# A planner that writes the instruction order of an attention and feed-forward kernel gets new costs, a replay as its judge, and two more late weight jobs

## The chip, the cores and the metric

One core of a Trainium2 chip runs the whole program, once per launch. The metric is the device time of one launch in microseconds (us), lower is better. TensorE (PE in the profile) does the matmuls, VectorE (DVE), ScalarE (ACT) and GpSimd (POOL) the elementwise work, and nearly every DMA is issued from one queue, that of SyncE (SP). PSUM has eight banks of 128 x 512 float32 values, into which matmuls accumulate.

## The reference, cut to what matters

```python
# q, k, v: (8, 8, 576, 64) float32.   w_in (512, 2048), w_out (2048, 512): float64
scores = q @ k.T / 8                            # per batch and head
mask: heads 0-3: 0 <= i - j < 32
      heads 4-7: 0 <= i - j < 128 and (i - j) % 4 == 0
attn = exp(scores - max);  attn /= attn.sum() + 1e-9
x = (attn @ v)  as 4608 tokens x 512
h = x @ w_in                                    # 4608 x 2048
g = maximum(h, 0) + log1p(exp(-abs(h)))         # softplus
out = g @ w_out                                 # 4608 x 512
```

Each row of scores has 32 live keys, so attention is small; the two matrix products of the feed-forward part are nearly all of the arithmetic.

## The kernel before, in words

**Tiling.** The 4608 tokens are nine chunks of 512 (`c` 0 to 8). A chunk's attention is four groups (a pair of heads each), taken as two *couples* of two groups. Everything is float32, and a large product is made of three matmuls: each factor is split into a high and a low part (`xh`, `xl`; `gh`, `gl`), and high x high, low x high and high x low accumulate in one bank. The splits are a copy with rounding on ACT and a subtraction on DVE. One matmul here is 128 x 128 weights by 512 columns.

**Stages.** (1) An *opening* of some 60 us whose order is written out by hand (`OPENING`). (2) The *early part*: chunks 0 to 2 in 48 slots (chunk, block of 128 of the 2048 hidden units), of which the planner orders slots 10 to 47. A slot is 12 matmuls into a bank `h_ps`, the softplus (three ACT steps, one DVE step), the split into `gh` and `gl`, and two slots later 12 matmuls into four banks `o_ps`. Beside it the weights, which come as float64 words, are decoded on ACT and DVE (`decode`). (3) The *late part*: chunks 3 to 8 as three pairs. For each pair both products are done by seven block products instead of eight (`PRODUCTS`): sums and differences of blocks of x (`s1` to `s4`) against sums and differences of blocks of the weights (`t1` to `t4`). One of 56 *units* of a pair is 12 matmuls into the banks `x`, `y` or `z`; units 0 to 27 (i = 0) are the first product, units 28 to 55 (i = 1) the second. Each unit's weights are one 512 KB tile of a ring of five (`load_ring`, tile `ring`), loaded from DRAM, where stage 2 left them.

**Jobs.** The blocks `t1` to `t4` are made by 16 *jobs* (`job(i, p, stage)`: product i, pair p of weight blocks). A job is two sums of 512 columns and four differences of 256, each of them on POOL or on DVE as the planner finds, then two copies on ACT and two subtractions on DVE (tiles `b`, `d`, `cast`) and four DMAs of 256 KB back to DRAM (`w_t<-cast`). Three jobs (`FIRST_JOBS`) run beside slots of the early part, nine more of stage 1 from the start of chunk 2 on; their `cast` tiles lie where ring tiles 3 and 4 will be. The last `LATE_JOBS` (4) of stage 2 come after `switch`, which hands the early part's memory to the late one; they use one set of tiles (`n1` to `n4`) one after the other, and the split tiles of units 28 to 30 come to lie on the same places.

**Couples.** `weights(n)`: load q and k, 128 small matmuls into one two-bank PSUM tile `att` (a PE *visit*), mask, maximum, 16 exponentials. `turned(n)`: `divisor`, a 32 x 32 transpose on DVE, four DMAs to DRAM and one back (`send`, `bring`; `turned<-sq`, `sq<-turned`). `attended(n)`: 128 small matmuls (a second visit), a division, a transpose, four DMAs out and one in (`send_x`, `bring_x`; `rows<-x_full`, `x_full<-rows`).

**What sets the order.** From slot 10 on, all work is a list of some two thousand `Task`s with an engine, a cost in us, and what it reads and writes. `prioritized` gives each a due time (`latest`), back from the planned begins of the PE chain; `simulated` runs the list, each engine taking the ready task with the earliest due time less its head start (`sooner`); a sum may go to POOL or, at another cost (`other`), to DVE. `blamed` lists the tasks behind each idle stretch of PE, the search gives some of them another head start, 400 times over (`PASSES`), keeps the plan whose simulated end is lowest, and writes the instructions in that order. So each engine runs in the planned order on the chip, and waits where the plan was too hopeful. Some costs carry `port`: DVE and POOL tasks with that mark never overlap in the plan; and a POOL sum that the plan held back gets a real wait on the DVE instruction that was ahead of it (`summed`, L913).

**Costs before.** `COST` gives a fixed part and a part for each column: ACT 0.22 + 0.00079 n, DVE 0.155 + 0.00104 n, POOL 0.05 + 0.00196 n, a PE matmul 0.2275; a DMA takes 0.1 us of SP; the queue moves 0.33 MB per us and lands 2.2 us later; a task on another engine starts 0.2 us after what it needs, on PE 0.6 us, a PE visit 1.5 us.

Of the kernel before, what the change touches and what calls it, by code (L numbers as in the profile page):

```python
# [51 lines left out]
NCP = NPAIR // 2  # L52
PLANNED = OPENED + 1
FIRST_JOBS = 3
LATE_JOBS = 4
RING = 5
NEG = -1.0e9
DEPTH = 8
# [43 lines left out]
def tile_windowed_attention_softplus_ffn(  # L102
# [497 lines left out]
    groups = [Group(c, pr) for c in range(NCH) for pr in range(NPR)]  # L600
# [42 lines left out]
    tiles, ready = {}, {}  # L643
# [202 lines left out]
    def load_unit(u):  # L846
# [4 lines left out]
        load_dma(out=ring[n].bitcast(F32), in_=streamed[i, PRODUCTS[k][1], jj])  # L851

    COST = {
        "PE": 0.2275, "ACT": (0.22, 0.00079), "DVE": (0.155, 0.00104), "POOL": (0.05, 0.00196),
    }
    LAST = len(slots) - 1
    PASSES, DEEP = 400, 12
    END, DMA_RATE, DMA_LATENCY, BACKLOG = 1.0e6, 0.33e6, 2.2, 2.0
    tasks, writer, readers = [], {}, {}

    class Task:
# [25 lines left out]
    def cost_of(engine, *widths):  # L887
        fixed, each = COST[engine]
        return sum(fixed + each * n for n in widths)

    def task(engine, widths, run, *what, reads=(), writes=(), **kw):
        widths = widths if isinstance(widths, tuple) else (widths,)
        return Task(engine, cost_of(engine, *widths), lambda: run(*what), reads, writes, **kw)

    def transfer(run, *what, size, n=1, reads=(), writes=()):
        return Task("SP", 0.1 * n, lambda: run(*what), reads, writes, size=size)

    chain = []

# [33 lines left out]
    TILE = 2 * P * CH * 4  # L933
# [39 lines left out]
    @sooner  # L973
    def weights(n, begun=False):
        x = x_of_couple(n)
        queries = ["q0", "q1"] if begun else [x]
        if not begun:
            transfer(load_queries, n, writes=queries, size=TILE, n=2)
            transfer(load_keys, n, writes=["k0", "k1"], size=TILE, n=3)
        Task("PE", 1.4, lambda: scores(n), [*queries, "k0", "k1"], ["att"], visit=True)  # L980
        for e in range(2):
            gr, s = groups[n + e], both("s") if e == 0 else [("s", 1)]
            task("DVE", (512, 512), gr.maximum, reads=["att"], writes=s)
            s = [("s", e)]
            for t in range(0, NB, 2):
                Task("ACT", 1.07, lambda gr=gr, t=t: gr.exponentials(range(t, t + 2)), (), s)

    @sooner
    def turned(n, begun=False):
        x = x_of_couple(n)  # L990
        if not begun:
            transfer(load_v, n, writes=both("v"), size=TILE)
        transfer(load_v, n + 1, writes=[x], size=TILE)
        for e in range(2):
            task("DVE", (8, 8), groups[n + e].divisor, reads=[("s", e)], writes=[("ri", e)])
            task("DVE", 512, turn, n + e, reads=[("s", e)], writes=[f"q{e}"])
            transfer(send, n + e, reads=[f"q{e}"], writes=[("sent", e)], size=TILE // 2, n=4)
            transfer(bring, n + e, reads=[("sent", e)], writes=[f"q{e}"], size=TILE // 2)

    @sooner  # L1000
    def attended(n):
        x = x_of_couple(n)
        Task("PE", 1.4, lambda: values(n), ["q0", "q1", *both("v"), x], ["att"], visit=True)
        for e in range(2):
            task(
                "DVE", 512, groups[n + e].normalized, reads=["att", ("ri", e)],
                writes=both("v") if e == 0 else [("v", 1)],
            )
        for e in range(2):
            task("DVE", 512, groups[n + e].turn_rows, reads=[("v", e)], writes=[x])  # L1010
        transfer(groups[n].send_x, reads=[x], writes=["rows"], size=TILE, n=4)
        transfer(groups[n].bring_x, reads=["rows"], writes=[x], size=TILE)

    def couples(first, last, begun=False):
# [102 lines left out]
    def decode(ff, i, n):  # L1117
        key = ff, i
        a, w = ("a", n % 3), ("W", ff, i)
        task("ACT", 580, decode_step, *key, 0, reads=[], writes=[a])  # L1120
        for step in (1, 2):
            Task("DVE", 0.425, lambda step=step: decode_step(*key, step), (), [a])
        for step in (3, 4):
            task("DVE", 512, decode_step, *key, step, writes=[a], port=True)
        task("ACT", 512, decode_step, *key, 5, reads=[a], writes=[w])
        task("DVE", 512, decode_step, *key, 6, reads=[a], writes=[w], port=True)

    def early_slot(i):
        c, ff = slots[i]
        turn = i % 2  # L1130
        h, e, gh, gl = ("h", turn), ("early e", turn), ("early gh", turn), ("early gl", turn)
        on_tensor(12, h_unit, i, reads=[("W", ff, 0), *x_keys(c)], writes=[h])
        o_unit(i - LAG)
        task("ACT", (512, 512, 512), activated, i, reads=[h], writes=[e])
        task("DVE", 512, softplus, i, reads=[h], writes=[e])
        task("ACT", 512, g_high, i, reads=[e], writes=[gh])
        task("DVE", 512, g_low, i, reads=[e, gh], writes=[gl], port=True)
# [222 lines left out]
    for i in range(2):  # L1360
        for p in range(NPAIR):
            for b in ("b11", "b21", "b22"):
                transfer(
                    keep_block, i, p, b, reads=[("W", 2 * p, i), ("W", 2 * p + 1, i)], writes=[("D", i, b, p)],
                    size=TILE // 2,
                )
    couples(2 * NPAIR - 8, 2 * NPAIR - 4, True)
    kept_first = slots.index((0, 6)) + LAG
# [1 line left out]
    for i in range(PLANNED, LAST + 1):  # L1370
# [3 lines left out]
        if slots[i] == (2, 0):  # L1374
# [5 lines left out]
            couples(2 * NPAIR - 4, 2 * NPAIR)  # L1380
            for n in range(FIRST_JOBS, 2 * NPAIR - LATE_JOBS):
                sooner(job, JOBS_SOONER)(n // NPAIR, n % NPAIR, 1)
# [5 lines left out]
    for i in range(LAST + 1 - LAG, LAST + 1):  # L1388
# [5 lines left out]
         + both("e0") + both("e1") + [("n", n) for n in range(1, 6)] + [("n", 1, 1)])  # L1394
    for p in range(NPAIR - LATE_JOBS, NPAIR):
        sooner(job, JOBS_SOONER)(1, p, 2)
    for u, (s, i, k, jj) in enumerate(units):
# [10 lines left out]
        else:  # L1408
            x = PRODUCTS[k][0]
# [7 lines left out]
    def simulated():  # L1417
        free = dict.fromkeys(("PE", "POOL", "DVE", "ACT", "SP", "NONE"), 0.0)
        candidates = {e: [] for e in free}
        queue_free = port_free = 0.0  # L1420
        for t in tasks:
            t.left, t.ready, t.chosen = len(t.after), 0.0, None
            if not t.left:
                candidates[t.engine].append(t)
        order = []
        for _ in range(len(tasks)):
            best = None
            for e in free:
                some = candidates[e]
                if e == "DVE":  # L1430
                    some = some + [t for t in candidates["POOL"] if t.other is not None]
                if not some:
                    continue
                begins = [(max(free[e], t.ready, port_free if t.port else 0.0), t) for t in some]
                start = min(b for b, _ in begins)
                if e == "SP":
                    start = max(start, queue_free - BACKLOG)
                t = min((t for b, t in begins if b <= start), key=lambda t: (not t.visit, t.latest - t.sooner))
                if best is None or (start, t.latest - t.sooner) < best[:2]:
                    best = start, t.latest - t.sooner, t, e  # L1440
            start, _, t, e = best
            candidates["POOL" if t.other is not None else e].remove(t)
            order.append(t)
            t.chosen = e
            cost = t.other if t.other is not None and e == "DVE" else t.cost
            t.idle, t.begun, end = start - free[e], start, start + cost
            free[e] = end
            if t.port:
                port_free = end
            if t.size:  # L1450
                queue_free = max(queue_free, end) + t.size / DMA_RATE
                end = queue_free + DMA_LATENCY
            t.done = end
            for other in t.then:
                lag = 0.0 if other.engine == e else 1.5 if other.visit else 0.6 if other.engine == "PE" else 0.2
                other.ready = max(other.ready, end + lag)
                other.left -= 1
                if not other.left:
                    candidates[other.engine].append(other)
        return max(t.done for t in tasks), order  # L1460

    def prioritized(begins):
        for t in tasks:
# [22 lines left out]
    dice = random.Random(0)  # L1486
# [4 lines left out]

    def attempt():
        prioritized(begins)
        return simulated()[0]

    best = None
    for n in range(PASSES):
        tried = begins, [t.sooner for t in tasks]
        end = attempt()
        if best is None or end <= best[0]:  # L1500
            gaps = list(blamed())
            best = end, *tried, [t.begun for t in chain]
# [3 lines left out]
        for idle, late in dice.choices(gaps, weights=[g[0] for g in gaps], k=dice.choice((1, 1, 2))):  # L1506
            step = dice.choice((-5.0, 2.0, 5.0, 10.0, 20.0))
# [6 lines left out]
    taken = None  # L1514
    for t in simulated()[1]:
# [4 lines left out]
        if t.engine == "DVE" and t.port:  # L1520
            taken = pinned[0]
# [118 lines left out]
```

## Time and profile before

| what | us |
|---|---|
| median of three runs | 849.8 (849.76, 849.80, 851.98) |
| the profiled execution, whole | 847.29 |
| its span, first to last instruction | 845.5 |
| TensorE busy (matmuls) | 815.5 |
| VectorE, ScalarE, GpSimd busy | 633.6, 551.5, 253.8 |
| DMA | 218.95 MB, 259 GB/s over the span |

"Busy" counts an instruction from its start to its end as recorded. Ends and starts of neighbours overlap a little, so a chain of instructions is faster than the sum of their durations; and an instruction that waits for a port while it runs is counted busy. "Idle before" is the time that the engine stood still in front of an instruction, with what ended it.

### The profile page before, as it was taken

The numbers are of one execution on the slowest core, as the hardware profiler recorded it, in microseconds if no ns is written. First come the engines' busy times: TensorE is split into PE (matmuls) and PEld (weight loads), VectorE is DVE, ScalarE is ACT, GpSimd is POOL, SyncE is SP. The second block draws the span as 40 slices with busy tenths as digits, with TensorE's granted clock in tenths as the row PEclk, the third lists the DMA queues.
The fourth block names the chain that finished last, engine by engine and source line by source line (L and its number), as shares of the span: only waits on it lengthen the run. The fifth ranks groups of instructions, "written<-read, shape, count | busy, mean of one in ns | idle before, by whom it ended". The sixth has DMA issues, their size and how long they took to land.

```text
span 845.5 us, 19702 instructions
## 1 busy us (share of the span) xinstructions
PE 815.5 (96%) x7834; PEld 654.6 (77%) x7835; DVE 633.6 (75%) x874; ACT 551.5 (65%) x1185; POOL 253.8 (30%) x162
## 2 busy tenths in 40 slices
PE   6799999999999998999998999899999999999998
PEld 4678888888877876788877788688878888888886
DVE  5798898786766764788978867497888685666963
ACT  5687677775766854589976535688873527776341
POOL 0000000014642638563434304032164221322730
PEclk9899999999999999999999999999999999999999
DMA  9599992667887874999889997778778875555563
GB/s 331 182 315 382 336 307 89 193 203 249 287 293 247 282 232 125 328 338 326 295 267 300 350 357 267 282 246 295 242 272 298 295 233 195 199 196 183 195 230 118
DMA packets 118492, 218.95 MB, mean 259 GB/s; under 512 B 11520, under 2 KB 53632, under 8 KB 118400
## 3 DMA queue, kind: packets, MB, share of 16 engines
q1 hardware_dynamic: 117968, 216.97, 75.9%
q8 instruction: 62, 1.02, 0.5%
q10 hardware_dynamic: 432, 0.72, 0.2%
q14 instruction: 30, 0.25, 0.1%
HBM read 162.07 MB, written 55.57 MB: 257 GB/s over the span
## 4 chain that ended last, share of the span: by engine, by line
PE 86%; DVE 4%; DMA 4%; POOL 2%; issue 2%; ACT 1%; SPq 1%; DVEq 0%; POOLq 0%; ACTq 0%
PE y L215 23%; PE x L215 14%; PE z L215 14%; PE h_ps L215 14%; PE o_ps L215 14%; PE a_ps L215 3%; PE s_ps L215 3%; POOL b L913 1%; SPq L150 1%; DMA ring<-w_t 1%; DMA x_full<-rows 1%; DMA raw<-w 1%; DMA v<-vp 1%; POOL x_full L913 1%; DVE sm L423 1%
## 5 line engine op out<-in xcount | busy, mean ns | idle before, releaser
L913 POOL TENSOR_TENSOR g_of<-g_of 128x1024 f32<-128x1024 f32 x48 | 121.7, 2543 | 228.0 <-DVE g L913 135.4
L913 DVE TENSOR_TENSOR g<-g_of,g 128x1024 fp32r<-128x1024 f32 x84 | 127.1, 1526 | 43.0 <-ACT g L929 42.9
L929 ACT CAST g<-g_of 128x1024 fp32r<-128x1024 f32 x84 | 87.9, 1047 | 101.4 <-PE y L215 38.6
L215 PE MATMUL o_ps<-gh,parts 128*128 128x512 f32 x384 | 131.5, 401 | 0.3 <-issue 0.3
L215 PE MATMUL h_ps<-xh,parts 128*128 128x512 f32 x384 | 129.4, 395 | 0.0
L913 POOL TENSOR_TENSOR b<-parts 128x512 f32<-128x512 f32 x32 | 46.3, 1455 | 260.1 <-DVE parts L209 178.5
L215 PE MATMUL y<-g,ring 128*128 128x512 f32 x432 | 102.6, 395 | 2.5 <-DVE g L913 2.1
L1260 ACT ACTIVATE e<-e 128x1024 f32<-128x1024 f32 x96 | 101.8, 1061 | 2.6
L215 PEld LDWEIGHTS y<-g,ring 128*128 128x128 f32 x432 | 80.9, 188 | 22.1 <-DVE g L913 2.5
L215 PEld LDWEIGHTS o_ps<-gh,parts 128*128 128x128 f32 x384 | 72.6, 189 | 18.9 <-issue 0.7
L215 PEld LDWEIGHTS h_ps<-xh,parts 128*128 128x128 f32 x384 | 72.5, 189 | 16.5 <-DVE e L667 0.4
L215 PE MATMUL o_ps<-gl,parts 128*128 128x512 f32 x192 | 76.5, 399 | 2.7 <-DVE gl L682 2.6
L411 ACT ACTIVATE s<-s,nm 128x64 f32<-128x64 f32 x224 | 75.0, 336 | 4.0 <-DVE nm L402 3.9
L215 PE MATMUL h_ps<-xl,parts 128*128 128x512 f32 x192 | 75.3, 392 | 0.0
L215 PE MATMUL z<-g,ring 128*128 128x512 f32 x288 | 68.4, 395 | 1.7 <-DVE g L913 1.7
L215 PE MATMUL x<-g,ring 128*128 128x512 f32 x288 | 69.0, 395 | 0.6 <-issue 0.6
L215 PEld LDWEIGHTS z<-g,ring 128*128 128x128 f32 x288 | 53.9, 188 | 14.7 <-DVE g L913 2.1
L215 PE MATMUL x<-a_h,ring 128*128 128x512 f32 x192 | 64.5, 397 | 0.0
L215 PEld LDWEIGHTS x<-g,ring 128*128 128x128 f32 x288 | 53.7, 188 | 13.4 <-issue 0.8
L215 PE MATMUL z<-s_h,ring 128*128 128x512 f32 x192 | 63.4, 390 | 0.5 <-DVE ob L931 0.5
L215 PE MATMUL y<-s_h,ring 128*128 128x512 f32 x192 | 63.5, 392 | 0.3 <-DMA ring<-w_t 0.3
L913 DVE TENSOR_TENSOR g_of<-y,temp 128x512 f32<-128x512 f32 x60 | 39.2, 682 | 22.0 <-PE y L215 21.9
(96 smaller groups left out, 1518.7 us busy)
## 6 DMA issues: line engine op xcount, KB each, us to landing
ring<-w_t SPq DMA_DIRECT2D x96, 512.0 KB, 4.5
ring<-w_b SPq DMA_DIRECT2D x72, 512.0 KB, 4.4
raw<-w SPq DMA_DIRECT2D x64, 256.0 KB, 5.6
w_t<-cast SPq DMA_DIRECT2D x64, 256.0 KB, 4.4
w_b<-parts SPq DMA_DIRECT2D x48, 256.0 KB, 3.4
v<-vp SPq DMA_DIRECT2D x14, 512.0 KB, 5.3
x_full<-vp SPq DMA_DIRECT2D x14, 512.0 KB, 6.8
turned<-sq SPq DMA_DIRECT2D x112, 64.0 KB, 3.0
```

Source lines behind the costliest of these rows:

```text
L150: ins = tc.keep_in_program_order((engine or nc.sync).dma_start(**kw))
L215: tc.keep_in_program_order(nc.tensor.matmul(**kw))
L411: pin(nc.scalar.activation(out=self.blocks[:, t], in_=src, func=AF.Exp, bias=self.nm[:, t : t + 1], scale=1.0 / 8.0 if self.masked else 1. ...
L423: pin(nc.vector.tensor_scalar(out=sm, in0=sm, scalar1=1.0e-9, scalar2=1.0, op0=ALU.add, op1=ALU.mult))
L913: pin((nc.gpsimd if name == "POOL" else nc.vector).tensor_tensor(out=dst, in0=a, in1=b, op=op))
L929: pin(nc.scalar.copy(out=dst, in_=src))
L1260: pin(nc.scalar.activation(out=to(), in_=of(), func=func, **kw))
```

## The change

Four things change. **Costs** in the planner (`COST`, the exponentials, `divisor`, the first decode steps, the SP time of a DMA, the DMA rate; `divisor` and the first decode steps now carry `port`). **Lags**: 0.12 us on the same engine and 0.18 us across engines, 0.5 us to PE; a PE visit waits between 1 and 3 us after its inputs, by how much time it has (`calm`). **The judge**: a plan's order is run again by `replayed`, each engine in its fixed order, with random extra time on each task, twice, and the search keeps the plan with the lowest mean end of PE. **`LATE_JOBS`** goes from 4 to 6, so that seven jobs stay in stage 1. No instruction is added to or taken from the kernel: the order on each engine, the choice of POOL or DVE for the sums, and the place of two jobs are what can differ.

```diff
-LATE_JOBS = 4
+LATE_JOBS = 6
...
     COST = {
-        "PE": 0.2275, "ACT": (0.22, 0.00079), "DVE": (0.155, 0.00104), "POOL": (0.05, 0.00196),
+        "PE": 0.229, "ACT": (0.09, 0.00084), "DVE": (0.07, 0.00104), "POOL": (0.14, 0.00215),
     }
...
-    PASSES, DEEP = 400, 12
-    END, DMA_RATE, DMA_LATENCY, BACKLOG = 1.0e6, 0.33e6, 2.2, 2.0
+    PASSES, DEEP, SEEDS, CALM = 400, 12, 2, 3.0
+    SPREAD = {"PE": 0.0, "ACT": 0.02, "DVE": 0.02, "POOL": 0.05, "SP": 0.3, "NONE": 0.0}
+    LATE, VISIT = 0.3, 0.0
+    END, DMA_RATE, DMA_LATENCY, BACKLOG = 1.0e6, 0.38e6, 2.2, 2.0
...
-    def transfer(run, *what, size, n=1, reads=(), writes=()):
-        return Task("SP", 0.1 * n, lambda: run(*what), reads, writes, size=size)
+    def transfer(run, *what, size, n=1, each=0.4, reads=(), writes=()):
+        return Task("SP", each * n, lambda: run(*what), reads, writes, size=size)
...
-                Task("ACT", 1.07, lambda gr=gr, t=t: gr.exponentials(range(t, t + 2)), (), s)
+                Task("ACT", 0.67, lambda gr=gr, t=t: gr.exponentials(range(t, t + 2)), (), s)
...
-            task("DVE", (8, 8), groups[n + e].divisor, reads=[("s", e)], writes=[("ri", e)])
+            task("DVE", (8, 180), groups[n + e].divisor, reads=[("s", e)], writes=[("ri", e)], port=True)
...
-        transfer(groups[n].send_x, reads=[x], writes=["rows"], size=TILE, n=4)
+        transfer(groups[n].send_x, reads=[x], writes=["rows"], size=TILE, n=4, each=0.6)
...
-            Task("DVE", 0.425, lambda step=step: decode_step(*key, step), (), [a])
+            Task("DVE", 0.345, lambda step=step: decode_step(*key, step), (), [a], port=True)
...
-        task("ACT", (512, 512, 512), activated, i, reads=[h], writes=[e])
+        task("ACT", (560, 560, 560), activated, i, reads=[h], writes=[e])
...
-                    size=TILE // 2,
+                    size=TILE // 2, each=0.55,
...
-                lag = 0.0 if other.engine == e else 1.5 if other.visit else 0.6 if other.engine == "PE" else 0.2
+                lag = (
+                    0.0 if e == other.engine == "PE" else calm(other, end) if other.visit else 0.5 if other.engine == "PE"
+                    else 0.12 if other.engine == e else 0.18
+                )
...
+    def calm(t, ready):
+        return min(CALM, max(1.0, (t.latest - ready) * 0.15))
+
+    def replayed(order, seed):
+        dice = random.Random(seed)
...
+        for t in order:
+            t.met = t.held = None
+            if t.chosen == "POOL" and t.begun > t.ready + 0.1:
+                t.held = taken
+            if t.chosen == "DVE" and t.port:
+                taken = t
...
+                    for other in t.after if t.held is None else (*t.after, t.held):
...
+                        lag = 0.0 if e == other.chosen == "PE" else 0.2 if "PE" in (e, other.chosen) else 0.12
+                        start = max(start, other.met + lag)
...
+            cost = t.other if t.other is not None and e == "DVE" else t.cost
+            cost = cost * (1.0 + SPREAD[e] * dice.random()) + (LATE if dice.random() < 0.02 else 0.0)
...
+            if t.size:
+                queue_free = max(queue_free, end) + t.size / DMA_RATE
+                end = queue_free + DMA_LATENCY * (1.0 + 0.4 * dice.random())
+            t.met_at, t.met = start, end
+        return free["PE"]
...
     def attempt():
         prioritized(begins)
-        return simulated()[0]
+        order = simulated()[1]
+        return sum(replayed(order, seed) for seed in range(SEEDS)) / SEEDS
```

## Rows read from the trace of the kernel before

**Rows 1.** The page, part 1: busy time by engine, share, instructions.
```profile
PE 815.5 (96%) x7834; PEld 654.6 (77%) x7835; DVE 633.6 (75%) x874; ACT 551.5 (65%) x1185; POOL 253.8 (30%) x162
```

**Rows 2.** Windows by stage: length; busy (count) of five engines; PE clock; DMA share, GB/s.
```profile
56.00:262.00 206.00, 205.96 (x2004) 165.94 (x2006) 164.13 (x285) 147.82 (x366) 37.24 (x36) 1.00 0.80 266
262.00:338.00 76.00, 71.62 (x906) 57.05 (x891) 47.72 (x67) 45.78 (x120) 41.95 (x38) 0.98 0.67 209
338.00:422.00 84.00, 83.15 (x725) 67.50 (x724) 71.54 (x93) 68.77 (x134) 44.98 (x33) 1.00 0.93 323
```

**Rows 3.** PE's waits from 56 us on: total, times, longest, us.
```profile
PE s_ps L215 <- issue: 4.0, 1, 4.0
PE o_ps L215 <- DVE gl L682: 2.6, 1, 2.6
PE a_ps L215 <- DMA sq<-turned: 2.4, 2, 1.5
PE y L215 <- DVE g L913: 2.1, 1, 2.1
PE z L215 <- DVE g L913: 1.7, 1, 1.7
...
PE z L215 <- DVE ob L931: 0.5, 1, 0.5
PE y L215 <- DMA ring<-w_t: 0.3, 1, 0.3
```

**Rows 4.** Windows of 20 us, columns as in rows 2.
```profile
60.00:80.00 20.00, 20.00 (x271) 15.96 (x270) 17.94 (x38) 14.41 (x43) 0.00 (x0) 1.00 1.03 367
...
320.00:340.00 20.00, 17.39 (x70) 13.69 (x69) 10.58 (x10) 10.88 (x17) 17.01 (x14) 0.91 0.43 134
...
460.00:480.00 20.00, 19.39 (x205) 15.51 (x204) 18.42 (x21) 12.93 (x38) 9.61 (x4) 1.00 0.96 346
```

**Rows 5.** Timeline around two waits: start, us, engine, what, [idle before].
```profile
331.42 3.98 POOL L913 TENSOR_TENSOR b<-parts 128x512 f32<-128x512 f32 x2
332.48 1.77 DVE L682 TENSOR_TENSOR gl<-e,gh 128x512 fp32r<-128x512 f32 x1
444.01 7.12 POOL L913 TENSOR_TENSOR g_of<-g_of 128x1024 f32<-128x1024 f32 x3 [2.29 <-ACT g L929]
...
448.96 2.21 DVE L423 TENSOR_SCALAR sm<-sm 128x8 f32<-128x8 f32 x1
```

**Rows 6.** DVE's groups from 56 us on: divisor's first step, count, busy, mean ns.
```profile
L423 DVE TENSOR_SCALAR sm<-sm 128x8 f32<-128x8 f32 x30 | 19.8, 661 | 0.0
```

**Rows 7.** POOL's groups from 56 us on.
```profile
L913 POOL TENSOR_TENSOR b<-parts 128x512 f32<-128x512 f32 x32 | 46.3, 1455 | 260.1 <-DVE parts L209 178.5 <-DVE gl L682 36.3 <-DVE cast L1077 35.8
```

**Rows 8.** ACT's timeline, two neighbours back to back.
```profile
450.15 1.04 ACT L827 CAST a_h<-x_full 128x1024 fp32r<-128x1024 f32 x1
451.10 1.04 ACT L929 CAST g<-g_of 128x1024 fp32r<-128x1024 f32 x1
```

**Rows 9.** SP's timeline around 300 us: DMA issues.
```profile
300.15 5.49 SPq L150 DMA_DIRECT2D turned<-sq  x8
...
308.24 1.19 SPq L150 DMA_DIRECT2D sq<-turned  x2
```

**Rows 10.** POOL's timeline: first two sums of the first late job.
```profile
348.71 2.58 POOL L913 TENSOR_TENSOR b<-parts 128x512 f32<-128x512 f32 x2 [3.44 <-DVE s_l L831]
```

**Rows 11.** DVE's timeline: last subtraction of the last late job.
```profile
397.62 0.68 DVE L1077 TENSOR_TENSOR cast<-b,cast 128x512 fp32r<-128x512 f32 x1
```

**Rows 12.** PE's timeline: first matmuls of unit 28.
```profile
421.38 1.79 PE L215 MATMUL x<-g,ring 128*128 128x512 f32 x7
```

**Rows 13.** DMA from 338 to 422 us: total; issues, KB each, median us to landing.
```profile
DMA packets 11240, 27.15 MB, mean 323 GB/s; under 512 B 1248, under 2 KB 2400, under 8 KB 11232
...
ring<-w_t SPq DMA_DIRECT2D x15, 512.0 KB, 6.1
w_t<-cast SPq DMA_DIRECT2D x20, 256.0 KB, 5.7
```

More of the change, by code (lines that the diff above doesn't have):

```diff
@@ L1460, in simulated @@
         return max(t.done for t in tasks), order
+    def calm(t, ready):
+        return min(CALM, max(1.0, (t.latest - ready) * 0.15))
+    def replayed(order, seed):
+        dice = random.Random(seed)
+        engines = ("PE", "POOL", "DVE", "ACT", "SP", "NONE")
+        free, heads = dict.fromkeys(engines, 0.0), {}
+        queues = {e: [t for t in order if t.chosen == e][::-1] for e in engines}
+        queue_free = port_free = 0.0
+        taken = None
+        for t in order:
[4 more added lines that the diff above has]
+                taken = t
+        left = len(order)
+        while left:
+            best = None
+            for e in engines:
+                if not queues[e]:
+                    continue
+                t = queues[e][-1]
+                if e not in heads:
+                    start = free[e]
+                    for other in t.after if t.held is None else (*t.after, t.held):
+                        if other.met is None:
+                            start = None
+                            break
+                        lag = 0.0 if e == other.chosen == "PE" else 0.2 if "PE" in (e, other.chosen) else 0.12
+                        start = max(start, other.met + lag)
+                    if start is None:
+                        continue
+                    heads[e] = start
+                start = max(heads[e], port_free) if t.port else heads[e]
+                if best is None or start < best[0]:
+                    best = start, e
+            start, e = best
+            del heads[e]
+            t = queues[e].pop()
+            left -= 1
+            cost = t.other if t.other is not None and e == "DVE" else t.cost
+            cost = cost * (1.0 + SPREAD[e] * dice.random()) + (LATE if dice.random() < 0.02 else 0.0)
+            if t.visit:
+                cost += VISIT
+            end = free[e] = start + cost
+            if t.port:
+                port_free = end
+            if t.size:
[3 more added lines that the diff above has]
+        return free["PE"]
     def prioritized(begins):
```

## The prediction

> **What bounds the kernel now.** The first view is the busy time by engine: TensorE is busy 815.5 of 845.5 us [rows 1], so only its idle 30 us and its slow stretches can go. Second, busy time by stage: in the first 206 us under the planner PE is busy 205.96 us, so nothing is to be had there, and things can only go wrong; the idle time lies from 262 us on, 4.4 us of it up to 338 us and 0.85 us in the next 84 [rows 2]. The rest lies in the opening, which the change doesn't touch, behind the last matmul, and in later waits. Third, PE's waits from 56 us on [rows 3]. Seven of them are waits for other engines or transfers: 2.6 for the subtraction `gl`, 2.4 in two visits for the turned squares, 2.1 and 1.7 for splits `g`, 0.5 and 0.3; together 9.6 us. The longest one, 4.0 us, is "issue": it ends on nothing that another engine did, so no plan decides it. Last, the clock: in the slice with the 2.6 us wait the mean granted clock was 0.91 [rows 4]. With levels 1.0 (2.4 GHz) and 0.5 (1.2 GHz) that is 0.09 / 0.5 x 20 = 3.6 us at the low one, after PE had stood still, and costs 1.8 us. A plan can reach 9.6 + 1.8 = 11.4 us.
>
> **Where the waits come from.** POOL and DVE hinder each other: beside a run of POOL's sums a DVE step takes a multiple of its time. POOL's three sums at 444.01 ran 7.12 us, and in them `divisor`'s first step, 8 columns wide, took 2.21 us; `gl` at 332.48 took 1.77 us beside two sums of 3.98 us [rows 5]. Over the run the 30 first steps of `divisor` took 19.8 us, 0.66 each [rows 6]. The old plan prices both steps of `divisor` at 2 x (0.155 + 0.008) = 0.33 us with no port.
>
> **The change part by part.**
> *Prices.* A POOL sum of 1024 columns is 2.06 us by the old line, 2.34 by the new one; the trace has 7.12 / 3 = 2.37 [rows 5]. One of 512: 1.05 old, 1.24 new, 2.58 / 2 = 1.29 in the trace [rows 10], 1.46 in the mean with its waits [rows 7]. An ACT step of 1024: 1.03 old, 0.95 new; neighbours start 451.10 - 450.15 = 0.95 apart [rows 8]. An SP issue: 0.1 old, 0.4 new; eight took 5.49 us, 0.69 each, and two 1.19, 0.60 each [rows 9]. So a `send` with its `bring`, five issues, holds SP for some 3 us where the old plan had 0.5, which is more than the longest wait for squares (1.5) [rows 3, 9]. The plan was hopeful just where PE waited: on POOL, on the port, on SP. It was too cautious on ACT and DVE, and that caution goes: with ACT 8% and DVE some 10% cheaper, work is planned closer to its due time. That costs nothing where DVE has room (164 of 206 us in the first stage [rows 2]); without that cover one wait of the present kind comes there, 9.6 / 7 = 1.4 us, with a clock fall at most 3.2 us. On chip the prices themselves cost nothing: no instruction is added.
> *Visits.* They are put 1 to 3 us behind their inputs instead of 1.5. A visit that has time moves to where PE finds it ready; PE does units meanwhile. One without time moves nearer, to 1.0 us. From both sides: the 2.4 us for squares go, or as much comes again elsewhere; I take that they go, since SP's price alone covers both.
> *Judging by replays.* It runs before launch. Between nothing and all 9.6 us; it prefers plans in which a late task doesn't reach PE, and I give it the port waits, because port and order are now in it.
> *Six late jobs.* Two jobs leave the stretch 262 to 338, where POOL was busy 42.0 of 76 us [rows 2], and 17.0 of 20 in the slice of the 2.6 us wait [rows 4]. By the new prices a job is 2 x 1.24 + 4 x 0.69 = 5.2 us on POOL or 2.5 on DVE, plus 1.2 on DVE: up to 10.5 us of POOL go from there. The first loads of ring tiles 3 and 4, which need the places of the stage 1 tiles, can then start sooner (0.3 us), and the `gl` wait with its clock fall goes: 2.6 + 1.8 + 0.5 + 0.3 = 5.2 us. The price is in the next 84 us: POOL has 45.0 busy there [rows 2], so 10.5 us fit by time. The transfers are tighter: a job writes 4 x 0.262 = 1.05 MB, two make 27.15 + 2.10 = 29.25 MB [rows 13], 348 GB/s over 84 us. The nearest rows: 346 GB/s at a DMA share of 0.96, 367 at 1.03 [rows 4]. From both sides that is 79.7 to 84.5 us of transfers in 84: hidden, or 0.5 us too much, and no air. The new plan reckons with 380 GB/s, 77 us. I take it as hidden, because from 262 to 338 the queue moves only 209 GB/s [rows 2] and ring loads can go ahead by up to five units.
> The Trainium skill (SBUF — State Buffer, section "A bandwidth-pool intuition that's wrong") gives some 358 GB/s for a core's path to HBM. This case's trace differs: 367 GB/s over 20 us [rows 4]. By the page the new plan's 380 can't be had, and 29.25 MB would be 81.7 us; that speaks for the slower rival below, without deciding it.
>
> **Sum, against the profiled execution.** Gone: 9.6 + 1.8 = 11.4. Back: the replays know neither waits of the "issue" kind nor how long a transfer takes when the queue is full (6.1 us in the median for a ring tile from 338 to 422 us [rows 13], where an idle queue would have 0.4 + 1.4 + 2.2 = 4.0 by the plan's own numbers). I leave two new waits of the mean size, 2 x 1.37, and one clock fall of 1.8: 4.5 us. Net -6.9: 840.4 for an execution like the profiled 847.29. The three runs' median lies 2.5 us above that execution; carried over, 849.8 - 6.9 = 842.9.
>
> **The rivals.**
> *All of it goes* (11.4 us: 838.4). For: each of the seven waits has a mispriced cause. Against: this plan too is one draw, and transfers vary.
> *The waits only move* (849.8). The search ends after 400 tries as before, the margins on ACT and DVE are gone, and as many waits come in other places: seven of 1.4 us and one clock fall give the same sum. Against it: the old faults are systematic, and a port wait that is planned isn't a surprise.
> *The change doesn't do what it says.* Were the order nearly the same, the seven waits would stand and the time with them; with every price changed that isn't likely, and it counts with the case before.
> *Six late jobs don't fit before unit 28* (slower). The four late jobs ran from 348.71 to 398.30, one after the other on one set of tiles, 12.4 us each [rows 10, 11]. At that pace six end at 423.1, and the last transfer, 5.7 us [rows 13], lands at 428.8. Unit 28 began at 421.4, unit 30 some 5.6 us later, at 427.0 [rows 12]; its split tiles lie where the last job's `cast` tiles were and take 0.95 us on ACT [rows 8] and, by the new line, 1.14 on DVE: ready at 430.9, 3.9 us late, 5.7 with a clock fall. If the full queue holds up ring loads as well, 2.10 MB at 346 GB/s are 6.1 us more. So 5.7 to 11.8 lost, against 5.2 won up to 350 us, and the other 6.2 us of waits stay: +0.5 to +6.6, in the middle 853.4. It decides from the point where the last late transfer lands after about 424 us. For: the queue's 0.93 share and no air [rows 2]. Against: sums on DVE cost half of POOL's, and both the search and the replays see this chain.
>
> **How the numbers follow.** Three runs can tell about 0.3%, 2.5 us. Chances: the forecast 0.48 (its own range 839 to 847: between one and three new waits), all of it 0.14, the waits only move 0.17, slower 0.21. Faster 0.62, same 0.17, slower 0.21. The range goes from 836.5, 2 us under the full gain since an "issue" wait of 4.0 may fall away, to 853.5, the middle of the slower case; some 0.13 is left out.
>
> **What would show it.** Right: PE's waits from 56 us on without `gl` and without squares, some 3 us in all beside "issue"; `divisor`'s first step well under 0.66 us in the mean; no low clock between 320 and 340 us; the last late `cast` transfer landed before 424 us, with some of the late sums on DVE. Wrong: a wait of an `x` matmul near 421 us for `g` or for a ring tile, DMA share near 1 from 338 to 422; or new waits in the first 206 us, where there were none.

## The result: 836.4 us, nearly twice the forecast gain

| | median of four runs | range | profiled execution, its span |
|---|---|---|---|
| before | 849.78 | 847.86 to 851.98 | 847.29, 845.5 |
| changed | 836.41 | 833.63 to 838.43 | 835.70, 833.5 |

The ratio is 0.984, 95% interval 0.9802 to 0.9878: 13.4 us, where 6.9 were forecast. The time lies 0.1 us below the lower end of the range. The side was right, the size was not, and the experiments show that the division between late jobs and prices wasn't either.

The page of the changed kernel, part 1, answers to [rows 1]. PE's busy time fell by 3.5 us though it does the same matmuls. From 56 us on there are 3.4 us less of the low clock; matmuls at half speed there can account for 1.7 us of it, and the rest is not traced.

```profile
PE 812.0 (97%) x7835; PEld 654.1 (78%) x7835; DVE 619.3 (74%) x874; ACT 545.4 (65%) x1185; POOL 247.3 (30%) x162
```

Its windows by stage, columns as in [rows 2]. The idle 4.4 us from 262 to 338 are 0.3 now, with POOL busy 36 us there and not 42. The next 84 us hold 2.5 us of idle time, 334 GB/s and 49.7 us of POOL: the two jobs have arrived and fit.

```profile
56.00:262.00 206.00, 205.52 (x2221) 165.49 (x2220) 162.21 (x290) 146.39 (x371) 37.84 (x36) 1.00 0.81 269
262.00:338.00 76.00, 75.74 (x692) 61.28 (x691) 44.41 (x64) 49.51 (x121) 36.09 (x30) 1.00 0.67 217
338.00:422.00 84.00, 81.53 (x836) 66.49 (x835) 70.49 (x102) 68.57 (x151) 49.67 (x41) 0.98 0.95 334
```

PE's waits from 56 us on, to be read against [rows 3]: all seven waits of the kernel before are gone from their places. Three new ones have come: 2.5 us for `temp`, an eviction of a bank, near 388 us; 1.0 for `g` near 777 us; 0.3 for `gl` near 283 us.

```profile
PE y L215 <- DVE temp L915: 2.5, 1, 2.5
PE s_ps L215 <- issue: 2.1, 1, 2.1
PE y L215 <- DVE g L915: 1.0, 1, 1.0
PE h_ps L215 <- issue: 0.5, 1, 0.5
PE a_ps L215 <- DVE gl L682: 0.3, 1, 0.3
```

Windows of 20 us of the changed kernel, as in [rows 4]: no low clock any more from 320 to 340, and one where the wait for `temp` is.

```profile
320.00:340.00 20.00, 20.00 (x88) 16.28 (x87) 12.83 (x14) 11.44 (x17) 15.47 (x10) 1.00 0.56 184
380.00:400.00 20.00, 17.53 (x191) 13.87 (x191) 16.27 (x27) 17.74 (x41) 11.16 (x10) 0.91 0.98 352
```

DVE's group of `divisor`'s first step, against [rows 6]: 0.25 us in the mean, not 0.66.

```profile
L423 DVE TENSOR_SCALAR sm<-sm 128x8 f32<-128x8 f32 x30 | 7.6, 252 | 0.0
```

The same group with the port prices taken back (a_oldport_m, below): 0.65 us again. So it is the port prices that plan this wait away.

```profile
L423 DVE TENSOR_SCALAR sm<-sm 128x8 f32<-128x8 f32 x30 | 19.6, 653 | 0.0
```

### The profile page after: what moved, and what is told of

The parts are those of the page before. It is cut to its first block, busy times and chain, and to the rows that moved or that the text cites. A ratio compares the mean times of both kernels' runs of the same rounds, so it can differ in the third digit from the quotient of the medians.

```text
span 833.5 us, 19697 instructions
## 1 busy us (share of the span) xinstructions
PE 812.0 (97%) x7835; PEld 654.1 (78%) x7835; DVE 619.3 (74%) x874; ACT 545.4 (65%) x1185; POOL 247.3 (30%) x162
## 4 chain that ended last, share of the span: by engine, by line
PE 89%; DMA 4%; DVE 2%; ACT 1%; issue 1%; SPq 1%; POOL 1%; ACTq 0%; POOLq 0%
PE y L215 23%; PE z L215 15%; PE o_ps L215 15%; PE x L215 15%; PE h_ps L215 14%; PE a_ps L215 3%; PE s_ps L215 3%; DMA w_t<-cast 1%; DMA x_full<-rows 1%; SPq L150 1%; DMA raw<-w 1%; DMA mask<-msk 1%; DMA v<-vp 1%; POOL b L915 1%; PE t_ps L442 0%
## 5 line engine op out<-in xcount | busy, mean ns | idle before, releaser
L915 POOL TENSOR_TENSOR g_of<-g_of 128x1024 f32<-128x1024 f32 x48 | 116.0, 2421 | 237.1 <-DVE g_of L1265 150.9
L915 DVE TENSOR_TENSOR g<-g_of,g 128x1024 fp32r<-128x1024 f32 x84 | 139.5, 1672 | 42.3 <-ACT g L931 42.1
L215 PEld LDWEIGHTS o_ps<-gh,parts 128*128 128x128 f32 x384 | 71.9, 187 | 17.7
L411 ACT ACTIVATE s<-s,nm 128x64 f32<-128x64 f32 x224 | 75.0, 337 | 12.4 <-DVE nm L402 12.4
L215 PE MATMUL o_ps<-gl,parts 128*128 128x512 f32 x192 | 75.7, 394 | 0.0
L667 DVE SCALAR_TENSOR_TENSOR e<-h_ps,e 128x512 f32<-128x512 f32 x48 | 33.0, 687 | 43.9 <-ACT e L662 43.6
```

The lines of the kernel that those rows point to most:

```text
L215: tc.keep_in_program_order(nc.tensor.matmul(**kw))
L411: pin(nc.scalar.activation(out=self.blocks[:, t], in_=src, func=AF.Exp, bias=self.nm[:, t : t + 1], scale=1.0 / 8.0 if self.masked else 1. ...
L667: pin(nc.vector.scalar_tensor_tensor(out=e, in0=tiles.pop(i), scalar=0.0, in1=e, op0=ALU.max, op1=ALU.add))
L915: pin((nc.gpsimd if name == "POOL" else nc.vector).tensor_tensor(out=dst, in0=a, in1=b, op=op))
```

## Where the 12.0 us between the two spans are

The trace gives every idle stretch of PE with what ended it, and the stretches at the low clock. For all stretches over 0.2 us from 56 us on (the low clock costs half its length):

| us | before | changed | forecast: change | measured: change |
|---|---|---|---|---|
| waits for engines and transfers | 9.7 | 3.7 | 9.6 to 2.7: -6.9 | -6.0 |
| "issue" waits | 5.2 | 2.5 | 0 | -2.7 |
| cost of low clock | 3.4 | 1.7 | -1.8, +1.8: 0 | -1.7 |
| the rest of the span | 827.3 | 825.6 | 0 | -1.7 |

The whole executions differ by 11.6 us. The remaining 1.8 of the 13.4 are in the runs: the profiled execution of before stood 2.5 us under its median, that of the changed kernel 0.7 us. One profile of each kernel fixes these shares only roughly: a second one of before (before_again, below) has 10.9, 5.0 and 6.8 in the first three rows and 825.8 in the last.

**What the "issue" waits end on.** It can be read from the DMA records. In every kernel here queue q8 moved 62 packets of the kind "instruction", 16,384 bytes each (page of before, part 3):

```profile
q8 instruction: 62, 1.02, 0.5%
```

PE has some 15,900 recorded instructions, which make 62 groups of 256. The profiles of this document hold 37 "issue" waits of PE over 0.25 us from 56 us on. In 35 of them PE had come to one of a row of places in its order that lie whole multiples of 256 instructions apart (give or take one), and it went on 0.9 to 1.6 us after a q8 packet had landed. Its waits for engines and transfers, in the two kernels and b_seed1, lie at any distance. In before the longest of them splits a visit after 112 matmuls: PE stops at 534.21, a q8 packet starts at 535.65 and lands at 536.76, and PE goes on at 538.17. PE's timeline, and the DMA by queue from 535.6 to 535.7 us:

```profile
538.17 0.35 PE L215 MATMUL s_ps<-k,x_full 64*32 64x64 f32 x16 [3.96 <-issue]
```

```profile
q8 instruction: 1, 0.02, 69.1%
```

In the changed kernel PE waits at the same place in its order (the 11,714th instruction), also in a visit, but 2.1 us: the packet starts at 526.43, before PE stops at 526.94. PE's timeline, and the DMA by queue from 526.4 to 526.5 us:

```profile
529.00 0.34 PE L215 MATMUL s_ps<-k,x_full 64*32 64x64 f32 x14 [2.05 <-issue]
```

```profile
q8 instruction: 1, 0.02, 69.0%
```

So PE stands there until its next instructions have come; that the packets are PE's follows from their count, the places and the times, for no record names their engine. The plan sets what PE does at such a place and how fast it comes to it: a visit runs through 256 instructions in some 1.5 us, 128 large matmuls with their weights, 0.23 us each, need some 29. Plans that pass the 11,714th instruction without a wait had the packet 1.4 us or more earlier. Why a packet starts as late as at 535.65 is open.

## The experiments

All times are medians beside runs of the kernel before on the same chip; *a* is the changed kernel, *b* the one before. A *draw* is a plan from another seed of the search. The last four columns are from the profile, worked out as in the table above; "290-365" is the part of the waits for engines and transfers in that stretch. PE's idle time also counts in the low clock's length where the two overlap, which they do for 9 us or more in the two *a* kernels with four late jobs. "New prices" means all of the change but the late jobs: costs, lags, DMA rate and, but for a_oldjudge, the judge.

| kernel | late jobs | prices | us | ratio, 95% interval | waits | 290-365 | issue | low clock, us |
|---|---|---|---|---|---|---|---|---|
| before | 4 | old | 849.8 | | 9.7 | 4.9 | 5.2 | 6.8 |
| changed | 6 | new | 836.4 | 0.980 to 0.988 | 3.7 | 0 | 2.5 | 3.4 |
| before, profiled again | 4 | old | 850.3 (one run) | | 10.9 | 4.6 | 5.0 | 13.7 |
| b_seed1 | 4 | old | 851.8 | 0.998 to 1.005 | 9.9 | 6.5 | 5.4 | 13.7 |
| a_late4 | 4 | new | 849.9 | 0.997 to 1.002 | 17.7 | 16.1 | 0.8 | 23.9 |
| a_late4_seed1 | 4 | new | 850.1 | 0.998 to 1.002 | 16.7 | 13.6 | 0.6 | 20.5 |
| a_late5 | 5 | new | 836.5 | 0.982 to 0.989 | 5.4 | 4.1 | 1.8 | 3.4 |
| b_late6 | 6 | old | 845.2 | 0.991 to 0.997 | 7.8 | 2.6 | 6.1 | 6.8 |
| b_late6_seed1 | 6 | old | 835.6 | 0.981 to 0.988 | 5.7 | 1.8 | 0.7 | 0 |
| b_late6_seed2 | 6 | old | 840.5 | 0.985 to 0.995 | 8.8 | 3.7 | 1.6 | 6.8 |
| b_judge_late6 | 6 | old | 839.7 | 0.985 to 0.992 | 7.9 | 1.8 | 1.4 | 3.4 |
| a_seed1 | 6 | new | 833.1 | 0.975 to 0.983 | 4.3 | 0 | 1.0 | 0 |
| a_seed2 | 6 | new | 833.3 | 0.976 to 0.985 | 3.0 | 0 | 2.8 | 0 |
| a_oldjudge | 6 | new | 836.6 | 0.980 to 0.990 | 3.9 | 0 | 1.2 | 3.4 |
| a_visit15_m | 6 | new | 836.9 | 0.980 to 0.989 | 4.0 | 0 | 3.8 | 0 |
| a_oldport_m | 6 | new, port old | 838.7 | 0.980 to 0.990 | 7.0 | 0 | 3.8 | 0 |
| a_oldsp_m | 6 | new, SP old | 844.1 | 0.990 to 0.995 | 13.0 | 0 | 0 | 0 |
| a_late7 | 7 | new | 835.1 | 0.977 to 0.987 | 4.4 | 0 | 0.7 | 0 |

**Another draw of each planner.**

```diff
-    dice = random.Random(0)
+    dice = random.Random(1)
```

b_seed1: 

> The kernel before with another seed for the search (1 for 0), all prices old. Theory 'the old prices are wrong in a systematic way': another draw from the same planner has as many waits for engines and transfers from 56 us on, 7 to 13 us in all, and the time is 846 to 855 us. Rival 'luck of the draw': the time falls or rises by 8 us or more, as far as the change did.

a_seed1: 

> The changed kernel with another seed for the search. Theory 'the new prices and the replays find good plans': 833 to 842 us, waits for engines and transfers from 56 us on 2 to 6 us. Rival 'luck of the draw': 845 us or more.

851.8 and 833.1 us, both as the theories said: with one more plan of each planner, luck of the draw doesn't make the 13 us. The waits of b_seed1 sit in other places (3.7 for `s_l` near 352, 2.1 for a ring tile near 361) and come to the same sum.

**Late jobs alone, and all but the late jobs.**

```diff
-LATE_JOBS = 4
+LATE_JOBS = 6      # b_late6, in the kernel before
...
-LATE_JOBS = 6
+LATE_JOBS = 4      # a_late4, in the changed kernel
```

b_late6: 

> The kernel before with six late jobs and nothing else of the change. Theory 'prices': no more than 5 us are won (the gl wait with its clock fall near 334 us goes), port and queue waits stay elsewhere: 844 to 852 us. Rival 'the late jobs do it': below 841 us, with 262 to 338 us free of waits.

a_late4: 

> The changed kernel with four late jobs as before. Theory 'prices': 834 to 842 us, within 4 us of the changed kernel. Rival 'the late jobs do it': 843 us or more, with a wait for gl or a DMA between 300 and 345 us again.

a_late4_seed1 (the same with seed 1): 

> The changed kernel with four late jobs, another seed for the search. The first draw with four late jobs lost 14.3 us in one place: two PE visits at 346 to 358 us whose q and k were issued late, behind DMAs of `cast` tiles in SP's queue. Theory 'four late jobs leave nine for the stretch before 340 us, and any plan pays there': 842 us or more, again with its longest wait between 300 and 365 us. Rival 'a bad draw': 833 to 841 us, no wait over 3 us.

My theory said 834 to 842 us for a_late4; it took 849.9, and the second draw 850.1. With four late jobs the new prices win nothing, in two draws. PE's timeline of a_late4 shows it in one place:

```profile
345.77 1.17 PE L215 MATMUL s_ps<-k,x_full 64*32 64x64 f32 x64 [4.88 <-DMA x_full<-qp]
347.52 1.18 PE L215 MATMUL s_ps<-k,x_full 64*32 64x64 f32 x64 [0.58 <-DMA x_full<-qp]
357.52 2.04 PE L215 MATMUL s_ps<-k,x_full 64*32 64x64 f32 x128 [8.82 <-DMA k<-kdl]
361.40 0.76 PE L215 MATMUL x<-a_h,ring 128*128 128x512 f32 x1 [1.84 <-DMA ring<-w_b]
```

SP's timeline of a_late4 at that place, DMA issues:

```profile
344.71 1.83 SPq L150 DMA_DIRECT2D x_full<-qp  x4
350.04 3.30 SPq L150 DMA_DIRECT2D w_t<-cast  x4
353.44 0.90 SPq L150 DMA_DIRECT2D k<-kdl  x2
```

DVE's timeline of a_late4 there:

```profile
343.45 1.23 DVE L831 TENSOR_TENSOR s_l<-x_full,s_h 128x1024 fp32r<-128x1024 f32 x1 [3.32 <-ACT s_h L827]
349.32 0.69 DVE L1079 TENSOR_TENSOR cast<-b,cast 128x512 fp32r<-128x512 f32 x1 [4.64 <-ACT cast L1075]
```

The loads of q can start only when the last `s_l` of the first pair has read its place (343.45), and the loads of k stand in SP's queue behind four DMAs of a job whose `cast` was late (349.32). The old waits for `gl` and squares are indeed gone in this kernel; their 10 us came back as 14.3 at two neighbouring visits, with 23.9 us at the low clock. That these loads stood behind the job's DMAs is what the rows show; that the closer prices put the visits so near to them is argued only.

b_late6 won 3.8 us (845.2 against 849.0 beside it). From 262 to 338 us PE is busy 74.2 of 76 us (before 71.6, changed 75.7); what the plan keeps is in the first lines of PE's waits, an "issue" wait and two port waits for `g`:

```profile
PE s_ps L215 <- issue: 4.7, 1, 4.7
PE y L215 <- DVE g L913: 2.8, 1, 2.8
PE z L215 <- DVE g L913: 1.7, 1, 1.7
```

**The kernel before, profiled again.** before_again: 

> The kernel before once more, for a second profile. Theory 'an issue wait belongs to the plan': the wait of some 4 us of the second visit near 533 us is there again, with a low clock behind it, and the waits for gl, squares and g are within 1 us of the first profile's. Rival 'issue waits are chance': it is gone or below 1.5 us, or another visit has it.

PE's waits, four of its lines, against [rows 3]:

```profile
PE s_ps L215 <- issue: 4.7, 1, 4.7
PE a_ps L215 <- DMA sq<-turned: 4.4, 3, 2.3
PE o_ps L215 <- DVE gl L682: 2.6, 1, 2.6
PE z L215 <- DVE g L913: 1.6, 1, 1.6
```

The waits for `gl` and of `z` for `g` return to 0.1 us. The 2.1 us of `y` for `g` near 455 us don't return, against the theory; the waits for squares are 2 us longer, one of them (1.0 us, with a low clock) close ahead of that place. The "issue" wait is at the same visit again, 4.7 after 4.0 us, with 6.8 us of low clock behind it. So it is not chance: it comes with the program. Of the nineteen plans of this document eight wait 0.6 us or more at this place, b_late6 4.7 us and the changed kernel 2.1; eleven don't. The forecast's "no plan decides it" was wrong.

**Six late jobs with old prices, further draws and the new judge.** b_late6_seed1 (seed 1): 

> The kernel before, old prices and judge, with six late jobs and another seed for the search; the first draw took 845.2 us. Theory 'six late jobs alone win some 4 us': 841 to 848 us, and less than b_seed1's waits between 300 and 365 us. Rival 'its 4 us were the draw': 849 us or more, as the other seed gave with four late jobs.

b_late6_seed2 (seed 2): 

> The kernel before, old prices and judge, six late jobs, a third seed. Two draws took 845.2 and 835.6 us. Theory 'the late jobs are the cause, prices add little': 834 to 846 us, and under 3 us of idle PE between 290 and 365 us. Rival 'the new prices are needed': 846 us or more.

b_judge_late6 (`replayed` and the new `attempt` put into the kernel before, old prices): 

> The kernel before with six late jobs and the replays as judge, at the old prices and lags. Theory 'prices': as with six late jobs alone, 842 to 850 us, since the replays use the same wrong prices. Rival 'the replays choose': 840 us or less.

845.2, 835.6, 840.5 and, with replays, 839.7. The theories for the seed 1 draw (841 to 848) and for the replays (842 to 850) missed; that for seed 2 holds in time, though not in its stretch (3.7 us of waits, not under 3). Each against the kernel before beside it, six late jobs are worth 4 to 15 us by themselves, 9 in the mean of the three draws without replays.

**Six late jobs with new prices: a third draw, and the old judge.**

```diff
-        order = simulated()[1]
-        return sum(replayed(order, seed) for seed in range(SEEDS)) / SEEDS
+        return simulated()[0]
```

a_seed2: 

> The changed kernel, a third seed; two draws took 836.4 and 833.1 us. Theory 'the late jobs are the cause, prices add little': 832 to 842 us, overlapping the old prices' draws with six late jobs. Rival 'the new prices make the plan safe against the draw': within 833 to 837 us again.

a_oldjudge: 

> The changed kernel with the old judge: new prices, lags and six late jobs, but the search keeps the plan with the lowest simulated end, without replays. Theory 'prices and late jobs': 834 to 842 us. Rival 'the replays choose': 843 us or more, with waits of 7 us or more in all for engines and transfers from 56 us on.

833.3 us fits the theory and the rival, 836.6 the theory. Nothing that the replays decide stands out from the draws: 0.2 us with the new prices, 5.5 with the old ones. The draws with new prices (836.4, 833.1, 833.3) scatter by 3 us, with old ones by 10; their means are 834.3 and 840.4, and one old draw (835.6) lies among the new ones. Much of the old draws' scatter is "issue" waits, which no part of the change aims at. Taken off the profiled spans, with half of the clock falls that follow them directly, they leave:

| span less "issue", us | four late jobs | six late jobs |
|---|---|---|
| old prices | 838.6 and 840.1 (before, twice), 841.1 | 834.8, 833.6, 838.1 |
| new prices | 848.1, 846.6 | 831.0, 830.8, 827.4 |

By this table the late jobs alone win 4.7 us in the mean, the new prices behind them 5.8 more, and the new prices alone lose 7. It rests on one profile of each plan (two of before).

**Single prices taken back in the changed kernel.**

```diff
-"POOL": (0.14, 0.00215)         ->  (0.05, 0.00196); divisor without port=True   # a_oldport
...
-each=0.4 (0.6, 0.55)            ->  each=0.1                                     # a_oldsp
...
-calm(other, end) if other.visit ->  1.5 if other.visit                           # a_visit15_m
```

a_oldport: 

> The changed kernel with POOL's old price (0.05 + 0.00196 n) and without the port mark on the divisor; all else as changed. Theory 'the port prices removed the two waits for g': one or both come back (a unit of the second product waits 1.5 us or more for g near 450 or 620 us, as in every kernel with the old prices), 838 to 845 us. Rival 'six late jobs and the rest suffice': 833 to 838 us and no wait for g over 1.2 us.

a_oldsp: 

> The changed kernel with the old SP time of a DMA, 0.1 us each, in the planner; all else as changed. Theory 'SP's price removed the waits for squares': visits wait for squares or for q and k, 2 to 10 us in all, 838 to 848 us. Rival 'SP's price decides nothing': 833 to 838 us.

846.7 and 852.2 us, both beyond their theories, but neither tells of the price: in both plans the load of chunk 1's kept sums was written between the third and the fourth addition of chunk 0, and the Python name `obs[m]` already meant chunk 1's tile. The fourth addition went to that tile and waited for its load, and one block of chunk 0's output is without its addend. PE's and DVE's timeline of a_oldport there:

```profile
216.78 0.79 PE L215 MATMUL o_ps<-gh,parts 128*128 128x512 f32 x1 [6.71 <-DVE ob L1178]
216.03 0.69 DVE L1178 TENSOR_TENSOR ob<-o_ps,ob 128x512 f32<-128x512 f32 x1 [7.97 <-DMA ob<-kept]
```

SP's timeline of a_oldport around it, the load and the stores:

```profile
207.28 1.85 SPq L150 DMA_DIRECT2D ob<-kept  x4
215.27 1.82 SPq L150 DMA_DIRECT2D out_t<-ob  x2
```

With the tiles held by chunk both were run again, and the visits' lag as a third one:

```diff
-            out=obs[m], in0=o_ps[m], in1=obs[m], op=ALU.add
+            out=obs[c, m], in0=o_ps[m], in1=obs[c, m], op=ALU.add   # and wherever obs is read or set
```

a_oldport_m: 

> The changed kernel with POOL's old price and the divisor without its port mark, the kept sums' tiles held by chunk (without that the first run lost 6.7 us and a clock fall near 217 us). Theory 'the mix-up was most of its loss, the port prices are worth the two g waits': 836 to 840 us, a wait for g of 1.5 us or more near 620 us again. Rival 'the port prices are worth as much as SP's': 842 us or more.

a_oldsp_m: 

> The changed kernel with SP's old times, as before, but with the tiles of the kept sums held by chunk, so that the fourth addition of chunk 0 no longer goes to chunk 1's tile and waits for its load (5.1 us near 217 us with a clock fall of 6.8 us). Theory 'that mix-up made most of its loss': 7 to 9 us less than the 852.2 of the first one, 843 to 846 us. Rival 'SP's price': 850 us or more.

a_visit15_m: 

> The changed kernel with every PE visit planned 1.5 us behind its inputs as before, the kept sums' tiles held by chunk. Theory 'the visits' lag decides little beside late jobs and prices': 832 to 838 us. Rival 'later visits keep PE from waiting': 840 us or more, with 3 us or more of waits of visits for squares, q or k.

838.7, 844.1, 836.9 us, all as the theories said. Against the three draws of the changed kernel the plan without SP's price takes 8 to 11 us more, that without the port prices 2 to 6, that without the later visits 0 to 4; it is one plan each, and the draws scatter by 3. The prices of ACT and DVE, the lags and the DMA rate were not taken back singly. PE's waits of a_oldsp_m, six of its lines, are of every kind, with 1.3 of 13.0 us for squares:

```profile
PE x L215 <- DVE g L915: 2.9, 1, 2.9
PE y L215 <- DVE temp L915: 2.4, 1, 2.4
PE y L215 <- DVE g L915: 2.2, 4, 1.0
PE h_ps L215 <- DVE normal L540: 1.6, 1, 1.6
PE x L215 <- DMA ring<-w_b: 1.5, 1, 1.5
PE a_ps L215 <- DMA sq<-turned: 1.3, 2, 1.0
```

PE's waits of a_oldport_m hold the one of a `z` matmul for `g` near 617 us, which every kernel with the old port prices but b_seed1 has between 609 and 624 us, 1.6 to 2.5 us long; of those with the new ones only a_visit15_m has it, 0.7 us long:

```profile
PE z L215 <- DVE g L915: 2.5, 1, 2.5
```

**Five and seven late jobs.** a_late5 (`LATE_JOBS = 5` in the changed kernel): 

> The changed kernel with five late jobs. Theory 'each job that leaves the stretch before 340 us gives it time': between the two, 838 to 846 us, with a visit's wait for q and k near 345 to 358 us shorter than the 10.0 and 14.3 us of the two draws with four. Rival 'one job fewer is enough': 833 to 838 us and no such wait.

a_late7 (`LATE_JOBS = 7`): 

> The changed kernel with seven late jobs. Theory 'the stretch before 340 us is the narrow place and after it there is room': 832 to 839 us, as with five and six. Rival 'the late jobs crowd the next stretch': 842 us or more, with an x matmul near 420 us that waits for g or a ring tile.

836.5 and 835.1 us, one draw each. For five late jobs the theory (838 to 846) missed and the rival's time came: one job fewer before 340 us is enough, though a wait of 4.1 us for a ring tile stands near 347 us. Seven don't crowd the next stretch.

## Why the prediction was wrong in size

- *What bounds the kernel*: right. Taking off waits, "issue" and the low clock leaves 824 to 831 us of the span in all but the two *a* kernels with four late jobs. Between the two ends, a_seed2 and a_oldsp_m, 4.3 of 6.4 us come from the opening, which no run here touches: the 901st matmul on record begins at 54.2 and at 58.5 us.
- *Where the waits come from* (port, SP): right for the port, not shown for SP's part in the squares. The first step of `divisor` fell from 0.66 to 0.25 us; it and the `z` wait for `g` come back with the old port prices. With SP's old price waits of every kind come, but no more for squares (1.3 us) than a_late7 has with the new one (1.2). The Trainium skill (SBUF — State Buffer, section "SBUF: two separate sides") says that a GpSimd instruction and a VectorE instruction in a two-port mode or with two SBUF inputs hold a shared port pair in turn, each for its whole length; the 2.21 us step beside POOL's sums of 2.37 each [rows 5] agrees.
- *The step that failed first* is the sum's "issue": "it ends on nothing that another engine did, so no plan decides it". That no engine ended it was right; it ended on the packet with PE's next instructions, at a fixed place in PE's order where the plan had put a visit. The sum kept all of these waits, and it left out the clock fall behind the longest one: its "costs 1.8" is the fall near 334 us alone, while two windows of before show another, 0.09 / 0.5 x 20 = 3.6 us long:

```profile
520.00:540.00 20.00, 16.01 (x309) 12.70 (x308) 15.31 (x20) 13.46 (x28) 0.00 (x0) 0.96 0.92 341
540.00:560.00 20.00, 20.00 (x86) 16.41 (x85) 12.89 (x20) 15.42 (x30) 4.83 (x2) 0.95 0.73 224
```

  The "issue" waits fell by 2.7 us and the clock's cost by 1.7: 4.4 us of what the forecast lacked. Nothing in the change aims at them, so that they fell counts as luck of the draw; its other two draws have "issue" waits of 1.0 and 2.8 us.
- *The step that failed second* is the division of the gain: 5.2 us for the six late jobs, the rest for the prices, each by itself. In runs the late jobs alone won 4 to 15 us; with the "issue" waits taken off 4.7 in the mean, so their size was about right. The prices alone won nothing in two draws, and some 6 us in the mean once the jobs were late. The two don't add: with nine jobs before 340 us the new prices turn the old waits into a longer one.
- *Two new waits*: nearly right, three waits of 3.7 us in all for 2.7, and the one clock fall that was left for them came (1.7 us for 1.8).
- *The rest*: 1.7 us of the span have no cause here, no more than two profiles of before differ (1.5 us).
- *The slower rival* didn't come. The six jobs started at 335.31 and ended at 396.87, 10.3 us each and not 12.4; they started 13 us earlier than the four had, and ended 1.4 us earlier. POOL's timeline, their first sums, against [rows 10]:

```profile
335.31 3.63 POOL L915 TENSOR_TENSOR b<-parts 128x512 f32<-128x512 f32 x2 [1.16 <-DVE s_l L831]
```

DVE's timeline, the last subtraction, against [rows 11]:

```profile
396.14 0.73 DVE L1079 TENSOR_TENSOR cast<-b,cast 128x512 fp32r<-128x512 f32 x1
```

All their sums stayed on POOL; I had expected some on DVE. The DMA share rose from 0.93 to 0.95, and ring loads were not late.

## What to carry to other kernels

Where a planner writes the order, a wait that names no other engine can still belong to the program: profile it twice, see what returns in the same place, and look whether a packet of the instruction queue landed just before the engine went on. Such a wait can be lost with another plan. Before pricing a schedule better, ask which stretch holds more work than time: with the new prices, moving one job out of it won 13 us, and the new prices won something only behind such a move. Judge a change to a searching planner by several draws; here one plan more or less is worth up to 10 us.

## What was not expected of the hardware and the program

- "Issue" waits of 2 to 5 us come in the small-matmul visits (128 matmuls and as many weight loads in some 1.5 us), as at 538 us. They end 1.2 to 1.5 us after a 16 KB packet of PE's instructions has landed.
- A wait for transfers of one and the same program differs by 2 us between executions (squares: 2.4, then 4.4 us); of the port waits two return to 0.1 us, and one of 2.1 us doesn't.
- Two draws of the changed planner, 833.1 and 833.3 us, are faster than both kernels.
